# Attention and a gated feed-forward on one core: another written-out order, another table of engines, and a table of filler products

## The chip, the cores and the metric

One Trainium2 chip, one of its cores. A core has TensorE (products into PSUM, with its weight loads), VectorE, ScalarE, GpSimd and SyncE; here SyncE's queue issues all transfers between memory and SBUF. The metric is the device time of one execution in microseconds.

## What is computed

Four batches of causal attention with 12 heads, 448 positions and 64 features a head, and behind it a gated feed-forward that also mixes positions:

```
scores = q @ k^T / 8, masked above the diagonal;  attn = softmax(scores);  x = attn @ v   (heads side by side: 768)
h = relu(x @ w_in);  u, v = halves of h (512 each);  v_n = (v - mean) / sqrt(var + 1e-6)
v_s = w_spatial @ v_n + b_spatial (over positions);   out = (u * v_s) @ w_out
```

All inputs and the output are float32. Many operands are split into a high and a low part in a 16-bit type (or in the rounded 32-bit type), and three products of parts stand for one.

## The kernel before

The heads are taken in pairs, 24 in all, six to a batch. For a pair, q and k are loaded and turned; scores are taken; VectorE adds the mask and finds the negated maximum, ScalarE takes the exponential with its sum, the weights are normalised, turned, and multiplied with v (step kind A, "AV"), which gives a block of x^T. Pairs 0 to 9 turn q and k and the weights on TensorE in float32 (functions `qk_turn` and `wide`). Pairs 10 to 23 split q and k on VectorE, ScalarE or GpSimd (`scale_split`: a scaling in place, L513, a copy of the high part, L517, a subtract for the low part, L521 to L523), turn them with a transposing DMA and copy halves across (L849). After the sixth pair of a batch comes `ffn(b)`: per 128 positions a chain of 18 products for the half v (with ScalarE's evacuation to the tile hv at L1536, statistics on VectorE, a power on GpSimd, normalisation and split into vn at L1586 to L1595), four chains for u, four chains over positions (the spatial product wst x vn), and the output chains with w_out. A chain is cut into steps of three products (L1473). The weights w_in, w_spatial and w_out are loaded, decoded from 64-bit words and split in between.

All of it is written first as 2,496 steps in a list (`Plan.add`). Each has a number, the engine or engines it may run on with an assumed cost, the tiles it reads and writes, and a kind (T for turns, R and S for scores, A for AV, F, M and r for the feed-forward chains, X for a sum over partitions). Two tables then decide everything: `WHERE`, a letter for each step that may run on several engines, and `ORDER`, the sequence in which all steps are issued. `Plan.run` walks `ORDER`, takes tiles from small rings of buffers in that sequence (four banks ps, one px, three pf of PSUM; two qkT, two e, and so on) and keeps planned start times, in which a step of VectorE marked with `lock` and any step of GpSimd wait for one another. An engine runs its steps strictly in the sequence given.

TensorE also gets filler products (`plan.warm`, L689): a 128 x 128 by 256 product of a tile of ones into the third pf bank, whose result nobody reads. In the kernel before they are put in by planned times: while TensorE's planned time is under 46,000 ns and that bank is free, as many as fit in front of the next step. The trace has 32 of them, the last at 38.0 us.

Steps that the text names: 10 to 13 are the loads of pair 0 (q and k of either head), 72 to 75 those of pair 1; 14, 16, 18 and 20 turn pair 0's four pieces, 96 and 98 those of pair 1; 101 to 104 are the first scores of pair 0; 2373 is a subtract (L1593) for vn in the last batch.

Of the kernel before, what the change touches and what calls it, by code (L numbers as in the profile page):

```python
# [45 lines left out]
WARM, FILL = 46000, 107  # L46
# [3 lines left out]
    "AAADAAPPADAPPAPPPAPAAPDAAPAAPPAAPDPAPADDAPAADAAAPAAAPADDDAADAADAPDDDPAADAAPPAAAPDAPAPDAAADPADAPADDPAPDAAPPAAPD"  # L50
    "AAPADAPADPAPAPAPPAPAPPPPPPPAPAPADPPDAPPADPDPAPAPAPPPPAADAAAPAAADPPPPAPAPAPDDAADAAAAPDAPPDAPAPAPDAAPPDDAADAPAPA"
    "PADDAADDDAADADDAAAAAPPADSSAAAAADPDAAAAAPAAPDAADDDPDAPDAPSSPPDPPAPPDPAAAPAAAAAPPPAPAPDDDDADDAADPAPPAPADPADPAAPP"
    "SPPPPPPPPDPADPPDPADPPPDPPDDPPPAPDDPAPPPPDAPPAAPPPAPAADAPPPPPPAPAPAAAAAAAADAAPPPPDDPDPPSPPPDDDAPSPAPPPDPPSSPAAP"
    "PDPPPPADPPDDPADPPDDAADADPPPADAPPDDAAADDDA"
)
ORDER = (
# [141 lines left out]
class Plan:  # L198
# [38 lines left out]
    def run(self):  # L237
# [9 lines left out]
        busy = dict(FIRST)  # L247
        order, sent, ring, last = [], [], 0.0, None
        pool_end = dve_end = 0.0
        for n in ORDER:  # L250
            op = self.ops[n]
            e = op.at_engine
# [12 lines left out]
            if e == "PE":  # L265
                last = op.cls
                if busy[e] < WARM and (2, []) in free["pf"]:
                    now = max([busy[e], 2700] + [d.end + self.delay(d, e) if d.end else start for d in self.warm.deps])
                    while now + (fill := FILL if now > 6000 else 2 * FILL) < start - 40:
                        order.append((self.warm, e))  # L270
                        now += fill
# [1489 lines left out]
```

## Time and profile before

| | us |
|---|---|
| timed runs, median of 3 | 359.98 (358.84 to 360.11) |
| profiled execution, from its first to its last instruction | 358.6 |
| median of the timed runs above that span | 1.4 |
| TensorE busy, 2,602 products | 346.2 |
| VectorE / ScalarE / GpSimd busy | 285.9 / 268.7 / 161.6 |

The span is what the profiler saw of one execution; the timed runs are executions of their own. PE is TensorE, DVE VectorE, ACT ScalarE, POOL GpSimd, SP SyncE; SPq is SyncE's queue. A product counts as busy until its modelled end, so that two products close behind one another overlap and small gaps don't show.

### The profile page before, as it was taken

What the parts mean: (1) busy time and instruction counts of PE and PEld (TensorE: products, weight loads), DVE (VectorE), ACT (ScalarE), POOL (GpSimd) and SP (SyncE); (2) the same over time, 40 slices, a digit from 0 to 9 for tenths busy, and PEclk for the clock granted to TensorE, in tenths of its full rate; (3) what the DMA queues carried; (4) which work ended last, traced back from release to release, by engine and by line L of the source; (5) the groups of instructions that cost most, each with busy time, mean ns of one, the idle gap of its engine ahead of it and who ended that gap; (6) DMA issues with size and microseconds to landing.
All of it is one profiled execution on the core that took longest, in us unless ns stands there. A gap on an engine that the chain in (4) does not pass through costs nothing.

```text
span 358.6 us, 8098 instructions
## 1 busy us (share of the span) xinstructions
PE 346.2 (97%) x2602; PEld 225.5 (63%) x2602; DVE 285.9 (80%) x1116; ACT 268.7 (75%) x767; POOL 161.6 (45%) x223
## 2 busy tenths in 40 slices
PE   6999899999999999999999999999999999999995
PEld 5476555665555556765455579755755885555695
DVE  4899889999999999889898998987989994263420
ACT  3698899999999999888799989748789684231101
POOL 3133664337656468364374572334686710042400
PEclk9999999999999999999999999999999999999999
DMA  7959979746768999999997898997767978300014
GB/s 162 210 164 242 244 170 215 174 100 166 150 166 186 208 237 181 178 182 139 188 180 153 172 225 162 205 174 156 164 116 156 159 111 174 82 2 0 3 47 130
DMA packets 160796, 55.84 MB, mean 156 GB/s; under 512 B 155249, under 2 KB 156530, under 8 KB 160754
## 3 DMA queue, kind: packets, MB, share of 16 engines
q1 hardware_dynamic: 160754, 55.33, 74.5%
q8 instruction: 20, 0.33, 0.4%
q14 instruction: 22, 0.18, 0.1%
HBM read 26.76 MB, written 5.51 MB: 90 GB/s over the span
## 4 chain that ended last, share of the span: by engine, by line
PE 65%; DMA 10%; DVE 8%; ACT 7%; POOL 4%; issue 3%; SPq 2%; POOLq 0%; ACTq 0%; DVEq 0%
PE pf L1473 43%; PE px L1255 6%; DMA qkT<-qks 4%; PE ps L1021 3%; PE ps L934 3%; PE ps L1101 3%; ACT e L982 3%; PE ps L1102 2%; DMA et<-e 2%; PE ps L764 2%; POOL qks L523 2%; DVE ps L972 1%; DMA o<-in_moe_w_out_dram 1%; DMA wst<-wb 1%; ACT e L489 1%
## 5 line engine op out<-in xcount | busy, mean ns | idle before, releaser
L1473 PE MATMUL pf<-wi,xT 128*128 128x512 f16 (+1 forms) x360 | 61.6, 338 | 0.0
L1473 PE MATMUL pf<-xT,wi 128*128 128x448 f16 x288 | 59.3, 353 | 0.4 <-ACT hv L1536 0.4
L1124 ACT ACTIVATE ps<-ps,sm 128x384 f32<-128x384 f32 (+4 forms) x98 | 45.4, 463 | 13.2 <-DVE sm L1112 8.0
L1473 PE MATMUL pf<-wo,g 128*128 128x384 f32 x288 | 54.9, 341 | 0.0
L1213 DVE SCALAR_TENSOR_TENSOR e<-ps,sm,e 128x256 f16<-128x256 f32 (+4 forms) x98 | 46.3, 505 | 6.3 <-ACT e L489 6.3
L1473 PEld LDWEIGHTS pf<-wo,g 128*128 128x128 f32 x288 | 49.8, 188 | 2.0 <-issue 1.1
L489 ACT ACTIVATE e<-ps,sm 128x256 f16<-128x256 f32 (+4 forms) x98 | 44.3, 509 | 5.5 <-DVE sm L1146 1.9
L1112 DVE CUSTOM_DVE_ANT_0 ps<-ps,mask,sc 128x256 f32<-128x256 f32 (+4 forms) x98 | 47.2, 506 | 1.4 <-PE ps L1102 0.8
L1473 PEld LDWEIGHTS <-wi 128*128 128x128 f16 x288 | 27.4, 98 | 26.7 <-issue 3.0
L1473 PEld LDWEIGHTS <-xT 128*128 128x128 f16 (+1 forms) x360 | 27.2, 103 | 25.4 <-issue 4.7
L491 POOL TENSOR_SCALAR e<-e,sm 128x384 f32<-128x384 f32 (+3 forms) x43 | 23.8, 566 | 41.5 <-ACT e L982 13.6
L982 ACT ACTIVATE e<-ps,sm 128x256 f32<-128x256 f32 (+3 forms) x70 | 34.3, 500 | 4.6 <-DVE sm L972 2.6
L1473 PE MATMUL pf<-wst,vn 128*128 128x448 f16 (+1 forms) x176 | 36.0, 353 | 0.1
L523 POOL TENSOR_TENSOR qks<-qk,qks 112x512 f16<-112x512 f32 x21 | 24.2, 1157 | 20.3 <-ACT qks L489 8.9
L934 PE MATMUL ps<-qkT 64*128 64x128 f32 (+3 forms) x160 | 28.5, 444 | 0.9 <-ACT e L982 0.7
L1102 PE MATMUL ps<-qkT 128*64 128x256 f16 (+4 forms) x196 | 26.3, 284 | 0.4 <-DVE qkT L847 0.4
L1473 PEld LDWEIGHTS <-vn 128*128 128x128 f16 (+1 forms) x176 | 16.8, 98 | 15.2 <-issue 0.5
L1101 PE MATMUL ps<-qkT 128*64 128x256 f16 (+4 forms) x196 | 24.8, 291 | 0.9 <-DVE e L1213 0.7
L972 DVE CUSTOM_DVE_ANT_0 ps<-ps,e 128x128 f32<-128x128 f32 (+2 forms) x60 | 24.3, 441 | 1.2 <-PE ps L934 1.0
L1021 PE MATMUL ps<-ident,e 128*128 128x128 f32 x160 | 23.8, 279 | 1.3 <-POOL e L491 0.5
L1563 POOL TENSOR_TENSOR ln<-ln,mhalf 128x1 f32<-128x1 f32 (+1 forms) x16 | 10.6, 666 | 31.5 <-DVE ln L1555 26.8
L1021 PEld LDWEIGHTS ps<-ident,e 128*128 128x128 f32 x160 | 17.6, 141 | 9.1 <-issue 3.3
(168 smaller groups left out, 729.5 us busy)
## 6 DMA issues: line engine op xcount, KB each, us to landing
wb<-in_moe_w_in_dram SPq DMA_DIRECT2D x12, 512.0 KB, 4.3
vnat<-in_v_dram SPq DMA_DIRECT2D x24, 192.0 KB, 3.9
out_dram<-o SPq DMA_DIRECT2D x12, 384.0 KB, 3.0
qk<-in_k_dram SPq DMA_DIRECT2D x14, 224.0 KB, 4.0
qk<-in_q_dram SPq DMA_DIRECT2D x14, 224.0 KB, 4.2
o<-in_moe_w_out_dram SPq DMA_DIRECT2D x8, 384.0 KB, 4.1
qk<-in_q_dram SPq DMA_DIRECT2D x20, 112.0 KB, 4.8
qk<-in_k_dram SPq DMA_DIRECT2D x20, 112.0 KB, 3.6
```

The costliest lines, as they stand in the source:

```text
L489: nc.scalar.activation(out=dst, in_=src, func=AF.Copy, scale=scale)
L523: lambda e: HANDLE[e].tensor_tensor(out=dst_l(), in0=src(), in1=dst_h(), op=ALU.subtract),
L934: nc.tensor.matmul(out=at(bank)[r0:r0 + rn, o0:o0 + n], lhsT=flat32(t)[rows, q0:q0 + rn], rhs=k32(t)[rows, :n], start=True, stop=True, ski ...
L972: lambda e, ps=ps, n=n, u=u0 + u, sm=sm, o0=o0, h=h: nc.vector.tensor_tensor_reduce(out=at(ps)[:, o0:o0 + n], in0=at(ps)[:, o0:o0 + n], in ...
L982: lambda e, ps=ps, n=n, u=u0 + u, sm=sm, o0=o0, c=c: nc.scalar.activation(out=at(eb)[:, 128 * c:128 * c + n], in_=at(ps)[:, o0:o0 + n], fu ...
L1021: nc.tensor.transpose(out=at(pt)[:, 128 * i:128 * i + 128], in_=e32(at(eb))[:, c0 + i, :], identity=ident)
L1101: nc.tensor.matmul(out=o, lhsT=w, rhs=qkT[:, 2 + x, :n], start=True, stop=False)
L1102: nc.tensor.matmul(out=o, lhsT=w, rhs=qkT[:, 4 + x, :n], start=False, stop=True)
L1112: lambda e, ps=ps, n=n, u=u, sm=sm, o0=o0, m0=m0: nc.vector.tensor_tensor_reduce(out=at(ps)[:, o0:o0 + n], in0=at(ps)[:, o0:o0 + n], in1=m ...
L1124: nc.scalar.activation(out=dst, in_=src, func=AF.Exp, scale=-1.0, bias=at(sm)[:, u:u + 1], accum_out=at(sm)[:, 4 + 2 * u:5 + 2 * u],)
L1213: lambda e, part=part, src=src, sm=sm, u=u: nc.vector.scalar_tensor_tensor(out=part(1), in0=src(), scalar=at(sm)[:, 12 + u:13 + u], in1=pa ...
L1473: nc.tensor.matmul(out=o, lhsT=a(), rhs=rhs, start=(n0 + n == 0), stop=(n0 + n == len(mms) - 1), skip_group_check=len(out_ap()) > 1,)
```

## The change

It replaces the tables `WHERE` and `ORDER` by others and puts a table in place of the rule for fillers. The steps themselves, their dependencies, the rings of buffers and the rule of planned times are the same.

```diff
-WARM, FILL = 46000, 107
+FILLS = {
+    14: 3, 16: 1, 98: 1, 158: 5, 263: 5,
+}
...
-    "AAADAAPPADAPPAPPPAPAAPDAAPAAPPAAPDPAPADDAPAADAAAPAAAPADDDAADAADAPDDDPAADAAPPAAAPDAPAPDAAADPADAPADDPAPDAAPPAAPD"
...
+    "DDAAPPPAAPAAPDAPDDPAPPAAPPDAPPAAPAPDPAAADPAAAPAAPAAAPAPPDAPDAADAPDAPDPADAAPPDAPAAAPAAAPAADDPAAPPDDPAAAAAPPAAAA"
...
-                if busy[e] < WARM and (2, []) in free["pf"]:
-                    now = max([busy[e], 2700] + [d.end + self.delay(d, e) if d.end else start for d in self.warm.deps])
-                    while now + (fill := FILL if now > 6000 else 2 * FILL) < start - 40:
-                        order.append((self.warm, e))
-                        now += fill
+                if n in FILLS and (2, []) in free["pf"]:
+                    order += [(self.warm, e)] * FILLS[n]
```

Read out of the two pairs of tables: 197 steps run on another engine.

| steps on | before | after |
|---|---|---|
| VectorE | 932 | 910 |
| ScalarE | 547 | 546 |
| GpSimd | 228 | 248 |
| SyncE | 210 | 213 |
| TensorE (without fillers) | 579 | 579 |

The moves are 42 steps from ScalarE to GpSimd and 33 back, 39 from VectorE to ScalarE and 29 back, 30 from VectorE to GpSimd and 19 back, and five with SyncE. Beginning of two engines' sequences:

| | before | after |
|---|---|---|
| SyncE | 10, 73, 72, 75, 74, 12, 11, 13, 26, 22 | 73, 10, 12, 11, 13, 75, 95, 72, 22, 74 |
| TensorE | 14, 96, 98, 16, 18, 20, 101, 102, 103, 104, 105 | 14, 16, 18, 20, 101, 102, 103, 104, 96, 98, 105 |

A number in `FILLS` is that of the step in front of which the fillers stand. The first score step of a pair is TensorE's step number 123 (pair 8), 301 (pair 16), 400 (pair 20) and 466 (pair 23) before, and 114, 295, 384 and 454 after. From one TensorE step to the next the kind changes 203 times before and 179 times after; from F to A, R, S or M 22 times before and 12 after.

## Rows read from the trace of the kernel before

**Rows 1.** stretches of the span: busy us of each engine (instructions), TensorE clock, DMA

```profile
0.00:40.00 40.00, 35.28 (x264) 24.33 (x264) 31.80 (x135) 28.69 (x93) 12.76 (x39) 1.00 0.85 198
40.00:180.00 140.00, 136.50 (x1028) 81.60 (x1027) 128.27 (x515) 130.20 (x379) 76.18 (x100) 1.00 0.86 179
180.00:310.00 130.00, 129.97 (x1051) 88.43 (x1049) 108.69 (x433) 100.56 (x283) 61.67 (x72) 1.00 0.85 163
310.00:358.60 48.60, 44.48 (x265) 31.17 (x262) 17.09 (x35) 9.24 (x17) 11.03 (x14) 0.99 0.10 33
sum 358.60, PE 346.23 PEld 225.53 DVE 285.86 ACT 268.69 POOL 161.63; mean PE 86.56 PEld 56.38 DVE 71.46 ACT 67.17 POOL 40.41
```

**Rows 2.** TensorE's waits: who for whom, us in total, times, longest

```profile
PE ps L764 <- DMA qk<-in_k_dram: 1.0, 1, 1.0
...
PE pf L1473 <- ACT hv L1536: 0.4, 1, 0.4
```

**Rows 3.** timeline of TensorE at the start: start, us, line, tile, count, idle before

```profile
3.17 0.93 PE L738 MATMUL ps<-ident,qk 112*64 112x112 f32 x4 [1.31 <-DMA qk<-in_q_dram]
3.88 0.85 PE L689 MATMUL pf<-ones 128*128 128x256 f16 x3
4.59 0.98 PE L764 MATMUL ps<-ident,qk 112*128 112x112 f32 x4
...
8.88 0.77 PE L738 MATMUL ps<-ident,qk 112*128 112x112 f32 x4
9.49 0.27 PE L689 MATMUL pf<-ones 128*128 128x256 f16 x1
9.69 2.38 PE L934 MATMUL ps<-qkT 64*128 64x128 f32 x12
12.74 0.97 PE L934 MATMUL ps<-qkT 64*64 64x448 f32 x4 [0.68 <-ACT e L982]
13.65 0.50 PE L689 MATMUL pf<-ones 128*128 128x256 f16 x3
```

**Rows 4.** timeline of SyncE's queue at the start

```profile
0.80 1.46 SPq L701 DMA_DIRECT2D qk<-in_q_dram  x3
...
4.43 0.49 SPq L701 DMA_DIRECT2D qk<-in_k_dram  x1
```

**Rows 5.** DMA issues from 0 to 20 us: count, KB, us to landing

```profile
qk<-in_q_dram SPq DMA_DIRECT2D x8, 112.0 KB, 2.8
qk<-in_k_dram SPq DMA_DIRECT2D x6, 112.0 KB, 3.1
```

**Rows 6.** timeline of TensorE, a chain before half-array and before other products

```profile
53.35 0.81 PE L1473 MATMUL pf<-wi,xT 128*128 128x512 f16 x3
54.09 1.69 PE L934 MATMUL ps<-qkT 64*128 64x128 f32 x12
...
64.20 0.81 PE L1473 MATMUL pf<-wi,xT 128*128 128x512 f16 x3
64.85 0.93 PE L764 MATMUL ps<-ident,qk 112*128 112x112 f32 x8
```

**Rows 7.** the lines of subtract and copy on either engine: ns min/median/max

```profile
L523 POOL TENSOR_TENSOR qks<-qk,qks x21: 1147/1157/1164, 100.2 to 273.4; 112x512 f16<-112x512 f32 x21
...
L523 DVE TENSOR_TENSOR qks<-qk,qks x7: 674/682/920, 99.2 to 244.2; 112x512 f16<-112x512 f32 x7
...
L491 POOL TENSOR_SCALAR qks<-qk x8: 617/618/626, 142.0 to 258.6; 112x512 f16<-112x512 f32 x8
...
L487 DVE TENSOR_SCALAR qks<-qk x7: 417/421/1399, 133.8 to 272.9; 112x512 f16<-112x512 f32 x7
```

**Rows 8.** timeline of GpSimd and VectorE, two subtracts of the last batch

```profile
317.55 1.15 POOL L1595 TENSOR_TENSOR vn<-hv,vn 128x512 f16<-128x512 f32 x1 [0.94 <-DVE vn L487]
317.56 1.69 DVE L1595 TENSOR_TENSOR vn<-hv,vn 128x512 f16<-128x512 f32 x1
...
322.88 0.69 DVE L1595 TENSOR_TENSOR vn<-hv,vn 128x512 f16<-128x512 f32 x1
```

More of the change, by code (lines that the diff above doesn't have):

```diff
@@ L49 @@
 WHERE = (
-    "AAADAAPPADAPPAPPPAPAAPDAAPAAPPAAPDPAPADDAPAADAAAPAAAPADDDAADAADAPDDDPAADAAPPAAAPDAPAPDAAADPADAPADDPAPDAAPPAAPD"
[L51 to L54, printed above, removed]
+    "DDAAPPPAAPAAPDAPDDPAPPAAPPDAPPAAPAPDPAAADPAAAPAAPAAAPAPPDAPDAADAPDAPDPADAAPPDAPAAAPAAAPAADDPAAPPDDPAAAAAPPAAAA"
+    "ADDDAPPAAPAPAPAPPPPAPPPPPAPPPADAAPPAAPPADPAPAPAPAPPPPAADAAPPAAADPPAPPPAPPPADAAAAADAADAPPADPDADPADAPADAAADDPADA"
+    "AAADAPDDPAAAAADAAAADPPPDSSPPAAAPAAAAAPAAAPADAAPDDPAADPADSSPAPPPPPPPPPPPPAAAAAPPDPPDPPPAADAAADDAAPPPPSAPADPPDPP"
+    "SPPPPPPPAPPDPPDAPDPAPPPADPSAAPDPDDDSSAPPDPPPAPPPDAPDAAAPPDPDPPPPDAAAAADPPPPAPPPPPPPPPPSPAPPPPPPPPAAAPPPPSSPPPP"
+    "PPDPAAADPPADADPAADPDADAAPADPPPDPPDDAAAAAA"
 )
 ORDER = (
[127 rows of a table removed]
[128 rows of a table added]
 )
```

255 rows, old and new, of the table ORDER are left out of this document.

## The prediction

> **What bounds the kernel now.** I read the stretches of the span first, because the share of busy time differs from stage to stage. TensorE is busy for 346.2 of 358.6 us, and its idle 12.4 us lie in three places [rows 1]: 4.7 us before 40 us, 3.5 us in the 140 us from 40 to 180, 0.03 us from 180 to 310, and 4.1 us after 310, most of which is the last copy and store behind the last product. From 40 to 180 us ScalarE is busy 130.2 and VectorE 128.3 of 140 us, so there three engines run nearly full side by side; from 180 on TensorE alone is full. GpSimd has room everywhere (161.6 us busy in all). So a new sequence can gain only what TensorE loses: its start, the time between products of different kinds (busy in the profile, but not streaming), and its waits. Work taken off VectorE after 180 us is worth nothing by itself.
>
> Next the list of TensorE's waits, to see that no single one is large: 1.0 us for a k load near 39 us, 0.4 us for ScalarE's hv at 319 us [rows 2]. Then the first microseconds in the timeline [rows 3]. The first q transpose starts at 3.17 us, the second group only at 4.59, and the first score product of pair 0 at 9.69. Between stand the turns of pair 1 (steps 96 and 98) with fillers before them, and only then the other three turns of pair 0. Three fillers take 0.85 us at 3.88 and 0.50 us at 13.65: in the first ten microseconds TensorE streams at the lower level (1.2 GHz), afterwards at 2.4, although the clock column of rows 1 prints 1.00 for the whole stretch.
>
> **The change part by part.**
>
> *The start.* SyncE issues its first eight loads 0.49 us apart (1.46 us for three) [rows 4]. In the old order pair 0's four loads are the 1st, 6th, 7th and 8th, the last issued at 4.43 us; in the new one they are the 2nd to 5th, the last at about 0.80 + 4 x 0.5 = 2.8 us. They land 2.8 us (q) and 3.1 us (k) after their issue [rows 5], so the last of the four at about 5.9 us. The new order of TensorE turns pair 0 alone (14, 16, 18, 20), with one filler between where before there were nine and two turns of pair 1. A turn of four products takes about 0.75 us at the lower level (0.77 with its tail at 8.88 us). So the fourth turn starts near 6.2 and ends near 7.0, and the first scores start at about 7.2 us instead of 9.69: 2.5 us earlier. Not all of it stays. The twelve products of 101 to 104 took 2.38 us at the higher level [rows 3]. If the clock rises at the same 9.4 us (the filler at 9.49 is the first short one, 0.27 us), the first 2.2 us of them run at half pace and do 1.1 us of the work; the rest ends at 9.4 + 1.3 = 10.7 instead of 12.07 us. That is 1.4 us earlier. Bounds: 2.5 us gained if VectorE's reading of the scores is what counts, and 1.2 us lost if the clock stays low until 20 us (a rival, below). I take a gain of 1.5 us. It goes through to the end because everything up to 40 us hangs on this first softmax: the two turns of pair 1 then fill TensorE's wait for it (0.68 us idle at 12.74 and fillers at 13.65) instead of standing in front.
>
> *The fillers.* 32 before, 15 after. A filler is free where the next product waits anyway. At the higher level one costs 0.11 us (three in 0.50 us with a tail of 0.27). All 17 dropped ones in the way would be 17 x 0.11 = 1.9 us, none in the way 0. They stand in front of products that wait, so I take 0.3 us.
>
> *Changes of kind.* Decoded from the two orders, TensorE changes from one kind of step to another 203 times before and 179 times after. Three 512-column products of a chain followed by transposes start the next thing after 0.65 us (64.20 to 64.85); followed by score products on half the rows, after 0.74 us (53.35 to 54.09) [rows 6]: 0.09 us for such a change, nothing for the other. Changes from a full chain to half-array steps (scores, AV, the narrow hv chain) fall from 22 to 12: 10 x 0.09 = 0.9 us. Bounds: nothing, and 24 x 0.09 = 2.2 us if every change costs that. I take 0.9.
>
> *Work moved between engines.* VectorE runs 22 steps fewer, GpSimd 20 more, ScalarE 1 fewer, SyncE 3 more. With the medians of each form on each engine (the like of rows 7) VectorE loses 13 us of work, GpSimd gains 22, ScalarE loses 1. A subtract in qks is 0.68 us on VectorE and 1.16 on GpSimd; the f16 copy before it 0.42 and 0.62 [rows 7]. From 40 to 180 us, where it could matter, ScalarE's load stays the same within 0.5 us and VectorE's falls by some 4 of 128: relief, but ScalarE is as full as before, so I count 0. Above 180 us TensorE hides it. The three extra across copies on SyncE are one issue of about 0.5 us each in a queue that mostly waits; 0, and 1.5 us at worst.
>
> *The shared port.* At 317.56 us VectorE's subtract takes 1.69 us beside a GpSimd subtract that began at 317.55, and 0.69 us without one at 322.88 [rows 8]. ScalarE's hv, and with it TensorE at 319, comes late by it: the 0.4 us of rows 2. The new table gives this subtract (step 2373) to GpSimd. I count the 0.4 us as gone. The GPSIMD Engine Reference of the Trainium skill (section 8, Key points) says that GpSimd shares its SBUF interfaces with VectorE and contends with instructions that have two SBUF inputs. The trace agrees by the 1.69 us, and the rule speaks against 22 us more of GpSimd's work; if each microsecond held VectorE up, VectorE would end with 9 us more and not 13 less, still below TensorE's total, and the sum would stay.
>
> *Other waits.* The 3.5 us idle between 40 and 180 us can go, or come again at other places, for nearly every product there has new neighbours: between -3.5 and +3.5 us. I take 0.
>
> Sum against the profiled span: 358.6 - 1.5 - 0.3 - 0.9 - 0.4 = 355.5 us. The median of the timed runs is 1.4 us above that span (359.98), so 356.9 us.
>
> **The rivals.**
>
> *New waits eat the gain (no change).* The new order brings attention forward: the first score step of pair 20 is TensorE's step 384 instead of 400, of pair 8 step 114 instead of 123. ScalarE must deliver the same exponentials earlier while it is 93% busy from 40 to 180 us [rows 1]. For it: only some 10 us of idle ScalarE to draw on. Against it: from 180 us on, products of the feed-forward part cover TensorE without a gap. If TensorE waits 3 us more between 40 and 180, the time is 359.9 us.
>
> *The clock stays low (no change).* With 5 fillers instead of 11 in the first 9.5 us, and otherwise transposes, the higher level may come later. Between 9.69 and 20 us TensorE did about 7 us of real products; at half pace from 7.2 us on they take 14 and end at 21.2, so the start is 1.2 us late instead of 1.5 early: 356.9 + 2.7 = 359.6 us. Slower than before by more than can be told only if the low level lasted to about 24 us. Against it: in rows 3 the level rose after a stretch that was mostly transposes. The page TensorE: Matmul & The Clock Gate of the Trainium skill (Part 4) says that transposes do not count as TensorE's activity; by it the rise would wait for the score products, which start at 7.2 us here. No row separates the two, since fillers and transposes alternate.
>
> *GpSimd becomes late (slower).* For pairs 19 to 21 the new table puts nearly the whole splitting of q and k on GpSimd. With rows 7 one pair's copies and subtracts for q and k cost 2 x (0.62 + 1.16) = 3.6 us there, 2 x (0.42 + 0.68) = 2.2 on VectorE, plus the scaling: about 1.8 us later per pair, in a queue where the normalising of others stands behind. Then comes a transposing DMA, then the scores. If the cover before the scores is shorter than that, TensorE waits: four pairs at 1.8 us are 7 us, 356.9 + 7 = 364 us. For it: GpSimd's forms are half as fast, and its share from 180 to 310 us goes from 47% to about 57%. Against it: TensorE waits 0.03 us there now, with long chains between. It decides from where the pair's operands land after its score step is due.
>
> That the change does less than it says (no filler, because the third feed-forward bank is taken at those steps) costs nothing in this sum.
>
> **How the numbers follow.** Forecast 0.58; new waits 0.16 and the clock 0.09, both no change; GpSimd late 0.13; other mishaps of the new neighbours, slower, 0.04. What a measurement here can tell from no change is about 0.5%, 1.8 us. Faster 0.58, within 0.25, slower 0.17. The range: below, all of the start (2.5), the changes of kind (2.2) and some of the idle 3.5 us give 353.3; above, the no-change cases and one pair's worth of lateness, 359.9 + 1.8 = 361.7. The forecast's own range is 353.3 to 358.2.
>
> **What would show it.** Right: the first half-array score product near 7.2 us; TensorE's busy total some 2 to 3 us smaller; no wait at the spatial products of the last batch; VectorE near 273 us and GpSimd near 184 us busy; TensorE without a gap from 180 to 310 us. Wrong: fillers or transposes at the low pace after 12 us; waits of scores for qkT between 200 and 290 us; more than 5 us idle from 40 to 180 us, ended by ScalarE.

## The result, and the profile after

| | before | after |
|---|---|---|
| median, us | 358.73 (357.02 to 361.51) | 361.49 (359.08 to 363.98) |
| timed executions | 19 | 19 |

The ratio is 1.0071 with a 95% interval of 1.0054 to 1.0089: slower by 0.7%, some 2.5 us. A second comparison on another occasion gave 1.0066 (1.0045 to 1.0088). I had forecast 356.9 us, faster, with 0.17 for slower. That 361.49 us lies inside the range that I gave (353.3 to 361.7) is no merit: its upper end stood for one pair's worth of lateness of GpSimd in splitting q and k, which did not happen.

The two first profiles mislead: the span fell from 358.6 to 358.0 us. A timed execution lasts some 1.8 us longer than its span (360.98 with a span of 359.2, 357.29 with 355.4), so the profiled execution of before was one of the longest of its kernel and that of after one of the shortest. Executions of one kernel differ by some 2 us either way, so a difference of 0.7% is not to be read from one pair of spans; below I use several profiles of each side.

Two of the stretches of the changed kernel and the sums, in the columns of [rows 1]:

```profile
40.00:180.00 140.00, 136.35 (x1033) 83.60 (x1030) 132.34 (x510) 131.95 (x384) 84.76 (x108) 1.00 0.86 185
180.00:310.00 130.00, 129.01 (x1043) 87.79 (x1041) 104.06 (x422) 95.99 (x274) 65.35 (x80) 1.00 0.85 159
...
sum 358.00, PE 345.49 PEld 226.06 DVE 282.31 ACT 267.83 POOL 174.64; mean PE 86.37 PEld 56.51 DVE 70.58 ACT 66.96 POOL 43.66
```

From 40 to 180 us VectorE rose by 4.1, ScalarE by 1.8 and GpSimd by 8.6 us; I had VectorE fall there. More profiles confirm VectorE (128.3 to 129.5 us busy in three profiles of the old tables, 131.8 to 133.1 in four of the changed ones) and not ScalarE (130.2 to 132.5 against 131.4 to 132.5: the same). From 180 to 310 TensorE, gapless before, lacks 1.0 us. TensorE's longest wait after the start, from the answer to [rows 2]:

```profile
PE px L1255 <- DVE xT L1277: 0.7, 1, 0.7
```

Several of half a microsecond follow it. But the kernel before has such waits too, beside the two in rows 2:

```profile
PE ps L1101 <- DVE e L1213: 0.7, 2, 0.3
PE ps L1021 <- POOL e L491: 0.5, 1, 0.5
```

The places are new and the sizes are not: from 40 to 180 us TensorE is idle 3.65 us (140 - 136.35), before 3.50. The start, the answer to [rows 3], TensorE with its weight loads (PEld) and then ScalarE:

```profile
3.93 0.93 PE L738 MATMUL ps<-ident,qk 112*64 112x112 f32 x4 [1.82 <-POOL e L650]
4.64 0.42 PE L689 MATMUL pf<-ones 128*128 128x256 f16 x1
4.86 2.67 PE L738 MATMUL ps<-ident,qk 112*64 112x112 f32 x12
7.46 3.62 PE L934 MATMUL ps<-qkT 64*128 64x128 f32 x12
...
11.15 0.61 PEld L764 LDWEIGHTS ps<-ident,qk 112*128 112x128 f32 x4 [1.22 <-ACT e L982]
11.99 0.39 PEld L764 LDWEIGHTS ps<-ident,qk 112*128 112x128 f32 x4 [0.17 <-ACT e L982]
12.55 0.20 PEld L934 LDWEIGHTS ps<-qkT 64*64 64x64 f32 x4 [0.17 <-ACT e L982]
10.19 0.47 ACT L982 ACTIVATE e<-ps,sm 128x256 f32<-128x256 f32 x1 [2.08 <-DVE sm L972]
...
11.83 0.58 ACT L982 ACTIVATE e<-ps,sm 128x384 f32<-128x384 f32 x1
...
14.40 0.63 ACT L982 ACTIVATE e<-ps,sm 128x448 f32<-128x448 f32 x1 [0.48 <-DVE sm L993]
```

And ScalarE in the kernel before:

```profile
11.78 0.37 ACT L982 ACTIVATE e<-ps,sm 128x128 f32<-128x128 f32 x1 [2.29 <-DVE sm L972]
...
12.14 0.47 ACT L982 ACTIVATE e<-ps,sm 128x256 f32<-128x256 f32 x1
...
14.60 0.64 ACT L982 ACTIVATE e<-ps,sm 128x448 f32<-128x448 f32 x1
```

Pair 0's scores start at 7.46 us (forecast 7.2) and its first exponential 1.59 us earlier than before (10.19 against 11.78). Its last one, over 448 columns, starts only 0.20 us earlier (14.40 against 14.60). The lead goes at TensorE. A turn or a score needs one of the four ps banks, and pair 0's first scores hold them until ScalarE's exponentials give them back. Before, the 448-wide scores took the first bank that came free, behind the second exponential (12.14 + 0.47 us; they start at 12.74, rows 3). Now the two turns of pair 1 stand in front of them and take the first two banks, at 11.15 and 11.99, and the scores get the third, behind the fifth exponential (11.83 + 0.58 us): they start at 12.55, 0.19 us earlier than before. From there to their exponential it is 1.85 us, before 1.86. ScalarE's copies of pair 1's turns (0.98 us at 12.38) are not on this path: behind them ScalarE stands 0.48 us for VectorE. Of the lead that I counted as lasting to the end little is left within 5 us.

The stall at 319 us [rows 2, 8] is gone. GpSimd has both subtracts now, 4 us apart (316.70 and 320.67), and TensorE's first wait there is 0.22 us, for a third one:

```profile
316.70 1.15 POOL L1595 TENSOR_TENSOR vn<-hv,vn 128x512 f16<-128x512 f32 x1 [2.07 <-DVE vn L487]
...
320.67 1.15 POOL L1595 TENSOR_TENSOR vn<-hv,vn 128x512 f16<-128x512 f32 x1
...
323.84 1.12 PE L1473 MATMUL pf<-wst,vn 128*128 128x448 f16 x5 [0.22 <-POOL vn L1595]
```

What the stall hung on I had read wrongly. ScalarE's hv in the kernel before started when GpSimd's own subtract ended (317.55 + 1.15 = 318.70 us), not with VectorE's slowed one (317.56 + 1.69 = 319.25):

```profile
318.74 0.69 ACT L1536 ACTIVATE hv<-pf,inv 128x512 f32<-128x512 f32 x1 [1.21 <-POOL vn L1595]
```

**VectorE beside GpSimd.** The slowing itself matters elsewhere. Around 41 us GpSimd of the changed kernel splits w_in, and VectorE's normalising copy of a 128x128 block of e takes 1.17 us beside it (GpSimd and then VectorE); the same form takes 0.27 us in the kernel before, at 22.97 (second block):

```profile
41.37 3.53 POOL L523 TENSOR_TENSOR wi<-wa,wi 128x512 f16<-128x512 f32 x3
40.73 0.84 DVE L487 TENSOR_SCALAR wi<-wa 128x512 f16<-128x512 f32 x1
41.48 1.17 DVE L487 TENSOR_SCALAR e<-e,sm 128x128 f32<-128x128 f32 x1
42.58 0.67 DVE L1277 SCALAR_TENSOR_TENSOR xT<-px,vsc,xT 128x448 f16<-128x448 f32 x1
```

```profile
22.97 0.27 DVE L487 TENSOR_SCALAR e<-e,sm 128x128 f32<-128x128 f32 x1
```

With the copy before it (0.84 us, a form that otherwise takes 0.42) VectorE loses 1.3 us there, and its next result, xT, is what TensorE waits for 0.69 us at 43.30. All nine profiles with the changed tables up to 75 us have these two slow copies, none of the six with the old tables there has. For the stretch from 40 to 180 us I counted each instruction of VectorE at the median of its form in the old tables (the sums exceed the stretch, as instructions overlap). So counted, its work fell from 167.4 to 163.5 us (means of three and four profiles), as forecast; but what its instructions took above these medians rose from 0.9 to 5.9 us, all of it in instructions during which GpSimd worked.

**Where the time goes.** Both kernels do the same steps on TensorE in other orders, so I compare the times at which the same amount of work is done: each step counts with the 15th percentile of the intervals from such a step to the next, over the kernels compared. The rows say how much later than in one profile of the kernel before with 15 fillers (span 355.5) a stretch of work is passed. The first three kernels have the old tables, the last four the changed ones (those named hoist have some products of TensorE moved; see below).

| TensorE's work, us (time in the run) | before | 15 fillers | hoist_8 | after | again | hoist_early4 | hoist_7 | new tables minus old, means |
|---|---|---|---|---|---|---|---|---|
| 0 to 60 (to 75 us) | 1.17 | 0 | -0.97 | 1.49 | 2.16 | 2.56 | 1.62 | +1.9 |
| 60 to 145 (75 to 170) | 0.83 | 0 | 0.32 | -1.21 | -0.49 | -1.11 | -0.25 | -1.1 |
| 145 to 180 (170 to 205) | 0.92 | 0 | 0.76 | 2.03 | 1.91 | 2.32 | 1.84 | +1.5 |
| 180 to 320 (205 to 350) | 0.13 | 0 | 0.25 | 0.01 | -0.05 | 0.01 | -0.01 | -0.1 |

The sum, +2.2 us, is about what the two ratios say (2.5 and 2.4 us). The changed tables lose by 75 us, win back half of it by 170, lose again to 205, and from there nothing changes. All the profiles below, counted the same way, bear out the first loss: six with the old tables up to 75 us lie between -1.0 and 1.2, nine with the changed ones between 1.4 and 2.6. On average the changed ones are 0.7 us ahead at 18 us, 0.5 behind at 27 and still at 41, 1.0 behind at 43, right after the slow copies, and 1.7 at 75. The loss from 170 to 205 is less sure: seven profiles with old tables there lie between 0 and 1.2, ten with changed ones between 1.2 and 2.3, 0.9 apart on average.

### The profile page after: what moved, and what is told of

It reads as the page before. It is cut to its first block, busy times and chain, and to the rows that moved or that the text cites. A ratio compares the mean times of both kernels' runs of the same rounds, so it can differ in the third digit from the quotient of the medians.

```text
span 358.0 us, 8072 instructions
## 1 busy us (share of the span) xinstructions
PE 345.5 (96%) x2585; PEld 226.1 (63%) x2585; DVE 282.3 (79%) x1094; ACT 267.8 (75%) x766; POOL 174.6 (49%) x243
## 3 DMA queue, kind: packets, MB, share of 16 engines
HBM read 26.76 MB, written 5.51 MB: 90 GB/s over the span
## 5 line engine op out<-in xcount | busy, mean ns | idle before, releaser
L1473 PE MATMUL pf<-xT,wi 128*128 128x448 f16 x288 | 58.5, 353 | 0.0
L1124 ACT ACTIVATE ps<-ps,sm 128x256 f32<-128x256 f32 (+4 forms) x98 | 45.4, 463 | 16.6 <-DVE sm L1112 9.7
L1473 PE MATMUL pf<-wo,g 128*128 128x384 f32 x288 | 54.0, 340 | 0.0
L1213 DVE SCALAR_TENSOR_TENSOR e<-ps,sm,e 128x384 f16<-128x384 f32 (+4 forms) x98 | 45.3, 505 | 7.1 <-ACT e L489 6.9
L489 ACT ACTIVATE e<-ps,sm 128x384 f16<-128x384 f32 (+4 forms) x98 | 44.3, 509 | 3.5 <-DVE sm L1146 2.7
L491 POOL TENSOR_SCALAR e<-e,sm 128x128 f32<-128x128 f32 (+3 forms) x43 | 23.1, 549 | 36.0 <-DVE sm L993 15.4
L982 ACT ACTIVATE e<-ps,sm 128x128 f32<-128x128 f32 (+3 forms) x70 | 34.2, 499 | 6.2 <-DVE sm L972 5.4
L934 PE MATMUL ps<-qkT 64*128 64x128 f32 (+3 forms) x160 | 30.1, 463 | 0.3 <-ACT e L982 0.2
L523 POOL TENSOR_TENSOR qks<-qk,qks 112x512 f16<-112x512 f32 x22 | 26.2, 1200 | 8.6 <-DVE qks L487 4.4
```

The lines of the kernel that those rows point to most:

```text
L489: nc.scalar.activation(out=dst, in_=src, func=AF.Copy, scale=scale)
L523: lambda e: HANDLE[e].tensor_tensor(out=dst_l(), in0=src(), in1=dst_h(), op=ALU.subtract),
L934: nc.tensor.matmul(out=at(bank)[r0:r0 + rn, o0:o0 + n], lhsT=flat32(t)[rows, q0:q0 + rn], rhs=k32(t)[rows, :n], start=True, stop=True, ski ...
L982: lambda e, ps=ps, n=n, u=u0 + u, sm=sm, o0=o0, c=c: nc.scalar.activation(out=at(eb)[:, 128 * c:128 * c + n], in_=at(ps)[:, o0:o0 + n], fu ...
L1124: nc.scalar.activation(out=dst, in_=src, func=AF.Exp, scale=-1.0, bias=at(sm)[:, u:u + 1], accum_out=at(sm)[:, 4 + 2 * u:5 + 2 * u],)
L1213: lambda e, part=part, src=src, sm=sm, u=u: nc.vector.scalar_tensor_tensor(out=part(1), in0=src(), scalar=at(sm)[:, 12 + u:13 + u], in1=pa ...
```

## The experiments

All ratios are to the kernel before, timed on the same chip between the runs.

**The changed kernel again, and the fillers.** Theory: the tables bring new waits. Rival: with fewer fillers the clock rises late.

```diff
 before_newfill: the tables of before, with
-WARM, FILL = 46000, 107
+FILLS = {14: 3, 16: 1, 98: 1, 158: 5, 263: 5}
 after_fill14: the changed kernel, with
-    14: 3, 16: 1, 98: 1, 158: 5, 263: 5,
+    14: 11, 16: 3, 98: 1, 158: 5, 263: 5,
 after_oldrule: the changed tables, with the old rule (WARM, FILL) in place of FILLS: 80 fillers
 after_fillers_before: the changed tables, with the 32 fillers of before at the same steps
+FILLS = {14: 1, 96: 3, 98: 3, 16: 1, 18: 1, 20: 1, 101: 1, 157: 3, 158: 3, 159: 7, 137: 1, 194: 2, 261: 1, 263: 2, 291: 1, 49: 1}
```

> The changed kernel once more, for a second profile and more timed runs. If its loss lies in a start that differs from run to run (the clock theory), the span of this profile lies some 2 to 4 us above the first one of 358.0 us, the fillers and turns of the first 15 us run at the low pace for longer, and from 40 us on the steps stand at the same distances as in the first profile. If the loss is spread over waits between 40 and 310 us (the theory of new waits), the start is the same and the later steps come later by 2 to 3 us. Ratio to the kernel before: 1.005 to 1.009 by both.

> The tables of the kernel before, with only the 15 fillers of the new table (3, 1, 1, 5, 5 in front of the steps 14, 16, 98, 158, 263) in place of the 32. Clock theory: TensorE does less between 3 and 9.5 us, the higher level comes later, and the kernel is slower by 1 to 3 us (ratio 1.003 to 1.008). Theory of new waits: fillers stand in idle time, ratio 0.998 to 1.002.

> The changed tables with the old rule for fillers, which puts 80 of them into this order, 12 of these in front of or among the first eight TensorE steps. Clock theory: the higher level comes sooner and more surely, ratio to the kernel before 0.995 to 1.002 if the fillers behind 10 us cost little. Theory of new waits: ratio 1.005 to 1.010 as for the change, or more by what the added fillers stand in the way (0.11 us each, 7 us for all).

> The changed kernel with 11 fillers instead of 3 before its first turn and 3 instead of 1 before the second, so that TensorE is busy nearly without a gap from 1.3 us on. Clock theory: the higher level comes in the first score products or before them in most runs; ratio to the kernel before 0.996 to 1.003. Theory of new waits: ratio 1.005 to 1.009, like the change.

> The changed kernel with the 32 fillers of the kernel before, ahead of the same products of TensorE as there (14, 96, 98, 16, 18, 20, 101, 157, 158, 159, 137, 194, 261, 263, 291, 49), instead of its 15. In the kernel before, the exchange of 32 for 15 cost 0.9 us. If it costs as much here: 0.9 us faster than the changed kernel. If fillers only cost their own time where they delay a product that is ready: 0.5 to 1 us slower, as with 80 fillers (4 us).

| | us | ratio (95%) |
|---|---|---|
| after_again | 360.53 | 1.0066 (1.0045 to 1.0088) |
| before_newfill | 359.28 | 1.0025 (1.0003 to 1.0048) |
| after_oldrule, 80 fillers | 364.86 | 1.0187 (1.0164 to 1.0209) |
| after_fill14, 25 fillers | 361.12 | 1.0098 (1.0061 to 1.0136) |
| after_fillers_before, 32 fillers | 362.38 | 1.0089 (1.0066 to 1.0111) |

With ten fillers more at the first turns, the twelve scores run at the higher level, 2.26 instead of 3.62 us:

```profile
7.82 2.26 PE L934 MATMUL ps<-qkT 64*128 64x128 f32 x12
...
14.26 0.63 ACT L982 ACTIVATE e<-ps,sm 128x448 f32<-128x448 f32 x1 [0.64 <-DVE sm L993]
```

The 448-wide exponential starts at 14.26 instead of 14.40 us, and the kernel is not faster. The clock rival falls: the slow scores are real (the higher level came only about 4 us after their start) and cost nothing that these runs show. The first exponential starts 0.37 us earlier (9.82 against 10.19), but the 448-wide scores only 0.14 us earlier (12.41 against 12.55), for pair 1's second turn stands in front of them, and its k load, issued at 5.51, lands at 11.8 (the profile puts that turn's wait down to an exponential that had ended by 11.6). From these scores to their exponential it is 1.85 us again. The page TensorE: Matmul & The Clock Gate of the Trainium skill (Part 4: transposes are no activity) agrees with these two starts: sixteen products of turns with one filler among them, behind three fillers and 1.8 us of idling, left the level low; behind eleven fillers and 0.45 us of idling and with three fillers among them they did not. As the idling differs too, the two starts don't single the transposes out. Fewer fillers are not the whole loss: they cost 0.25% in the old sequence (interval to 0.48%) of 0.7%, and in the changed sequence more of them bring none of it back.

**Which part of the tables.** Cuts: the first N entries of one sequence with its engines, then all other steps in the order and on the engines of the other kernel. The fillers are those of the kernel that starts.

```diff
 frontN_after (N = 300, 690, 1075: to 42, 91, 138 us); frontN_before the other way round
-ORDER = OLD
+ORDER = NEW[:N] + [n for n in OLD if n not in NEW[:N]]
 WHERE: each step's letter from the kernel whose part of the order it stands in
 seq_before_eng_after: ORDER and fillers of before, with
-WHERE = OLD
+WHERE = NEW
```

> The first 690 entries of the sequence (to about 91 us) with their engines and the 15 fillers from the changed kernel, the other 1,810 entries and their engines from the kernel before. The kernel before is 358.0 here and the changed one 360.5. Theory 1, local waits in two places (28 to 60 us of TensorE's work, and 140 to 180): this part holds the first of them, 1.3 us, and 0.3 us at the start: 359.6. Theory 2, the start's waits are handed on and set off everything later: 360.5. Theory 3, the late half alone loses: 358.0 to 358.4.

> The other way round: the first 690 entries, their engines and the 32 fillers from the kernel before, the rest from the changed one. Theory 1 (two local places): only the late one is left, about 1 us, and 0.3 gained near the end: 358.9. Theory 2 (the start's waits handed on): 358.0. Theory 3 (the late half alone): 360.3.

> The first 1,075 entries (to about 136 us) from the kernel before with engines and fillers, the rest from the changed one. Theory 1: the waits at 175 to 205 us are in this rest, 1 to 1.3 us, but the 1.5 us that the changed kernel wins between 118 and 165 us are partly left out: 359.0. Theory 2: 358.0. Theory 3: 360.3.

> The whole sequence and the fillers of the kernel before, the engines of the changed one. If the loss comes from which engine does a step: 360 or more. If it comes from the sequence alone: 358.0. If each table only fits the other of its own pair: slower than both kernels, 362 and more, with new waits of TensorE on VectorE, ScalarE or GpSimd all over.

> Only the first 300 entries (to about 42 us) with their engines and the 15 fillers from the changed kernel; the rest from the kernel before. With 690 entries it was 2.5 us over the kernel before. If the early loss is made by 42 us (VectorE then stands 0.2 to 0.9 us for a weight load that lands at 35.8 us, and ends its casts a microsecond later): 2 to 2.5 us over again. If it is made from 45 to 75 us, where ScalarE is 98.6% busy in the changed kernel and 95% before: 0.5 to 1 us over, which is what the new fillers alone cost.

> The first 1,075 entries (to about 138 us) from the changed kernel, the rest from the kernel before: the stretch of 165 to 205 us is that of the kernel before. If the loss has two places, an early one and one of 1.3 us at 165 to 205 us: 1.2 us over the kernel before, that is 1.2 us faster than the changed one. If all of it is early and the late waits only follow from it: 2.5 us over, as the changed kernel.

> The first 1,625 entries (to about 206 us) from the kernel before, the rest from the changed one. In the traces nothing is lost after 205 us. If so: as the kernel before, within 0.3 us, or 0.2 to 0.4 us faster by the wait at 319 us that is gone. If the changed end (15 steps of VectorE and 12 of ScalarE given to GpSimd) is dear: 1 us over or more.

> The first 300 entries (to about 42 us), their engines and the 32 fillers from the kernel before, the rest from the changed one. If the loss of the changed kernel is in its start: 1.2 us faster than the changed one, 1.1 us over the kernel before. If the parts only fit their own other half: no faster than the changed one, 2.3 us over the kernel before or more.

| cut at | changed part first | changed part behind |
|---|---|---|
| 300 entries, 42 us | 360.21, 1.0039 (1.0018 to 1.0060) | 361.89, 1.0083 (1.0058 to 1.0108) |
| 690, 91 us | 361.09, 1.0072 (1.0052 to 1.0093) | 362.70, 1.0125 (1.0105 to 1.0145) |
| 1,075, 137 us | 365.18, 1.0153 (1.0120 to 1.0187) | 360.85, 1.0066 (1.0045 to 1.0086) |
| 1,625, 206 us | | 360.96, 1.0059 (1.0036 to 1.0081) |
| sequence before, engines after | 379.70, 1.0609 (1.0576 to 1.0643) | |

The parts don't add. At 690 they make 0.72 + 1.25 = 2.0%, the whole 0.7%. A cut can bring waits of its own at the seam; the one at 1,075 with the changed part first shows it as a single wait, between 130 and 160 us:

```profile
PE ps L1102 <- DVE qkT L847: 2.9, 1, 2.9
```

My theory of two local losses fails as a sum, most of all with front300_before, which should have won 1.2 us and won nothing, front1075_after (1.5% slower instead of 0.3) and front1625_before (0.6% slower instead of nothing, with its loss behind the seam). Two things hold: the changed start brings no gain (1.0039, with its lower bound above 1, of which its 15 fillers may be 0.0025), and the new table of engines is worth nothing on the old sequence (+6%; the new sequence with the old engines was not run).

**Filling the waits.** If the new waits of TensorE are themselves the loss, products that were ready before a wait began should fill it.

```diff
 after_hoist_early4: in ORDER, a product moved to just before the one that waits
+587 before 303, 588 before 428, 515 before 565, 606 before 375
 after_hoist_late3
+722 before 1074, 1208 before 1573, 1611 before 1684
 after_hoist_7: both
 before_hoist_8: in the ORDER of before
+349 before 440, 619 before 375, 649 before 662, 663 before 940, 664 before 935, 694 before 1098, 719 before 1074, 1172 before 1516
```

> The changed kernel with four products of TensorE moved to just before a product that waits, each of them ready before that wait began: 587 before 303 (wait of 0.68 us at 43 us), 588 before 428 (0.63 us at 50), 515 before 565 (0.31 us at 66), 606 before 375 (0.68 us at 87). Nothing else differs. The changed kernel was 2.5 us over the kernel before. If these waits cost what they last, the products fill them (0.65, 0.63, 0.2 and 0.65 us): 2.0 us faster than the changed kernel. If the chains of ScalarE and VectorE set the pace there (ScalarE 94% busy from 40 to 180 us), the wait only comes a product later: within 0.3 us of the changed kernel.

> The changed kernel with three products moved ahead in the same way: 722 before 1074 (waits of 0.52 and 0.42 us at 156 us), 1208 before 1573 (0.38 and 0.34 us at 182 to 183), 1611 before 1684 (0.63 us at 193). If the waits cost what they last: 0.55 + 0.57 + 0.4 = 1.5 us faster than the changed kernel. If VectorE and ScalarE set the pace: within 0.3 us of it.

> Both sets of moves, seven products. If each wait costs what it lasts: 3.5 us faster than the changed kernel, which is 1 us faster than the kernel before. If an early gain is handed on but the later waits end at times that other engines set: as the early four alone. If other engines set the pace all along: as the changed kernel.

> The kernel before with eight of its products moved ahead of waits of its own in the same way: 349 before 440 (0.71 us), 619 before 375 (0.63), 649 before 662 (0.30), 663 before 940 (0.50), 664 before 935 (0.41), 694 before 1098 (1.25 in the profiled execution, not in others), 719 before 1074 (0.35), 1172 before 1516 (0.27). The other half of the same question. If waits cost what they last: 2.5 to 3 us faster than the kernel before. If other engines set the pace: within 0.3 us of it. If the kernel before has such waits as large as the changed one's and they cost it nothing, the waits of the changed kernel are not the reason of its loss.

Measured: early four 361.76, 1.0099 (1.0068 to 1.0129); late three 361.32, 1.0081 (1.0056 to 1.0106); all seven 360.58, 1.0063 (1.0038 to 1.0088), where 3.5 us were to be gained if each wait cost what it lasts; before_hoist_8 359.16, 1.0008 (0.9990 to 1.0026), where it was 2.5. Nothing is gained on either side. TensorE in the changed kernel at the first of the waits:

```profile
43.30 2.04 PE L1255 MATMUL px<-et,vnat 128*64 128x448 f32 x14 [0.69 <-DVE xT L1277]
...
46.08 0.55 PE L1021 MATMUL ps<-ident,e 128*128 128x128 f32 x3
46.46 0.81 PE L1473 MATMUL pf<-wi,xT 128*128 128x512 f16 x3
47.11 1.57 PE L1021 MATMUL ps<-ident,e 128*128 128x128 f32 x12
48.52 0.93 PE L764 MATMUL ps<-ident,qk 112*128 112x112 f32 x8
```

and with the seven moves:

```profile
42.74 0.82 PE L1473 MATMUL pf<-wi,xT 128*128 128x512 f16 x3
43.52 2.04 PE L1255 MATMUL px<-et,vnat 128*64 128x448 f32 x14
...
46.30 2.61 PE L1021 MATMUL ps<-ident,e 128*128 128x128 f32 x15
48.74 0.93 PE L764 MATMUL ps<-ident,qk 112*128 112x112 f32 x8
```

The 0.69 us are gone. But the fifteen turns of weights behind now take 2.61 us where they took 0.55 + 1.57: their weight loads stand 1.0 us for ScalarE's exponentials and 0.5 us for GpSimd's normalising. The chain product had filled that time at 46.46. The next step starts 0.22 us later, not 0.65 earlier. That is how VectorE and ScalarE stand there too: xT starts at 42.80 instead of 42.58 and the 448-wide exponential at 47.48 instead of 47.25, and VectorE's slow copy takes 1.17 us as before. The wait of TensorE was the form in which the pace of VectorE and ScalarE showed, not the cause.

That ScalarE has next to no room from 45 us on, the stretches of the changed kernel say:

```profile
45.00:75.00 30.00, 29.39 (x239) 18.39 (x237) 28.61 (x108) 29.60 (x98) 16.05 (x24) 1.00 0.70 169
165.00:210.00 45.00, 44.04 (x343) 24.30 (x341) 38.78 (x158) 37.05 (x105) 26.92 (x34) 1.00 1.02 187
```

and those of before:

```profile
45.00:75.00 30.00, 29.46 (x231) 18.10 (x227) 27.34 (x103) 28.60 (x90) 14.05 (x22) 1.00 0.72 168
165.00:210.00 45.00, 44.66 (x351) 24.89 (x349) 40.53 (x162) 40.49 (x115) 23.58 (x28) 1.00 0.97 173
```

From 45 to 75 us ScalarE is busy 29.60 of 30 us (28.60 before) and VectorE 28.61 (27.34). From 165 to 210 it is the other way: ScalarE and VectorE have less to do, 37.1 and 38.8 against 40.5 and 40.5, GpSimd has 26.9 against 23.6, and TensorE 0.6 us less.

**GpSimd in the second stretch.** TensorE's weight loads wait for GpSimd's vn near 198 us, which they don't in the kernel before. Six splits of vn given back:

```diff
 after_split_back: WHERE of the changed kernel, but
-1138, 1153, 1168, 1183, 1184, 1185 on GpSimd
+1138, 1168 on VectorE; 1153, 1183, 1184, 1185 on ScalarE (as before)
```

> The changed kernel with six steps that split the normalised rows of the spatial products of the second batch (1138, 1153, 1168, 1183, 1184, 1185) on the engines of the kernel before (four on ScalarE, two on VectorE) instead of GpSimd; the sequence is the changed one. TensorE's weight loads wait 0.5 to 1.1 us for GpSimd there at 198 us. If GpSimd's lateness makes the loss of 165 to 205 us: 0.6 to 1.2 us faster than the changed kernel. If ScalarE and VectorE set the pace there anyway: no faster, or slower.

Measured: 368.66 us, 1.0250 (1.0214 to 1.0287), 1.8% above the changed kernel. The waits grow and move to other engines: from 202 to 208 us TensorE waits 1.24 us for VectorE's sc, 0.69 and 0.99 us for GpSimd's vn and 0.58 us for ScalarE's.

So giving these six steps back wins nothing; with this sequence they are better on GpSimd. What else GpSimd does there was not varied.

## Why the prediction was wrong

*What failed first: "It goes through to the end because everything up to 40 us hangs on this first softmax."* The 1.5 us were there (1.59 at the first exponential), and 0.2 were left at the last exponential of the same pair. TensorE's wait that the two turns of pair 1 were to fill was a wait for a ps bank, and the turns don't only fill it: they take the first two banks that come free, so that the 448-wide scores get the third and start 0.19 us earlier than before instead of 1.5. front300_after gives the sign: with the changed start alone the kernel is 0.39% slower (its 15 fillers included), not 1.5 us faster. I had also not seen that the first turn begins later (3.93 instead of 3.17 us; pair 0's first load is now issued second, at 1.25 us, and lands at 3.79; the row names a step of GpSimd that ends just then, the second profile names the load), which the scores at 7.46 still made good.

*What failed next: the shared port, "the sum would stay", and VectorE's load, "VectorE's falls by some 4 of 128: relief".* I took the slowing of VectorE beside GpSimd as 0.4 us at one place and looked only at VectorE's total. From 40 to 180 us VectorE's work at its usual durations did fall by some 4 us, but beside GpSimd, with 8.6 us more there, its instructions grew by 5 us, and VectorE ended busier (132.3 us against 128.3) in the stretch where TensorE hangs on it. At 41 us this is 1.3 us in front of the result that TensorE waits for, in every profile of the changed tables. That this slowing makes the loss is shown for that one wait in the traces; no run took GpSimd's work away there. For ScalarE the sentence ("the same within 0.5 us") holds over several profiles, though the first pair shows +1.8.

*What failed in size: other waits, "I take 0", with bounds of 3.5 us either way.* Against the old tables the stretches of work passed by +1.9, -1.1, +1.5 and -0.1 us, +2.2 us net, the lead of the start included. Little of it shows as idle time of TensorE (3.65 against 3.50 us from 40 to 180). The rival "New waits eat the gain" named the mechanism (attention brought forward onto a full ScalarE) and the stretch from 40 to 180 us, but at 0.16, and priced as no change; since there was no gain to eat, it came out slower.

*Fillers, -0.3:* a gain was forecast; 17 fewer cost 0.9 us in the old sequence (bounds 0.1 to 1.7). *Changes of kind, -0.9:* no row shows this gain, and no run tested it alone; TensorE's busy total, which was to fall by 2 to 3 us, is 345.5 and 344.9 in two profiles of the changed kernel and 343.5 in the old tables with the same 15 fillers. *The port at 319 us, -0.4:* the wait (0.38 us) is gone and one of 0.22 us stands in its place; and it had not hung on VectorE's slow subtract. Over the whole kernel VectorE's work at the medians fell by some 11 us, but what its instructions took above them rose by some 3 us (5 us from 40 to 180, less behind it) beside 13 us more of GpSimd: the GPSIMD Engine Reference of the Trainium skill (section 8, Key points: contention of the two engines) agrees. The totals were mis-sized: VectorE 282.3 us busy (forecast 273), GpSimd 174.6 (184).

*The rivals:* GpSimd late for pairs 19 to 21 did not happen; nothing is lost after 205 us, and the 1.0 us that TensorE lacks from 180 on lie before 200. The clock stays low did happen in part (scores of 3.62 us, the low level until about 11.7 us and not to 21) and cost nothing that the runs show.

*The base:* the sum was made against 358.6 us as if it were typical; the median execution of before has a span of about 358.7 - 1.8 = 356.9 us, so 355.5 us of span would have been a gain of 1.4 us and not of 3.1.

*What stays open.* Shown: most of the loss is in the tables and none was found in the clock; TensorE's new waits can be filled without gain; the changed start gains nothing, and why; VectorE is held up beside GpSimd; the loss arises by 75 us and, less surely, again from 170 to 205 us. That VectorE and ScalarE set the pace is shown in the traces for the first of the filled waits, at 43 us. How much of the loss comes from VectorE's slowing, and which steps of the tables bring the rest, is not shown: no run moved GpSimd's work at 41 us, and a cut adds waits of its own. No version tried beats the kernel before.

## What to carry to other kernels

Where three engines run at 90% and more, a wait of one engine is the place where another's pace shows: before counting an earlier start or a filled wait as gain, follow the same pair to its last instruction. Work that is moved into a wait takes buffers too: ask who gets the next one. Before work goes to GpSimd, ask which instructions of a full VectorE will run beside it. A written-out order and its table of engines belong together; the old order with the new engines was 6% slower. For a difference under 1%, take several executions of each side before reading one pair of profiles.

## What the runs showed of the hardware

The granted clock fell in the middle of a run. In after_split_back TensorE was busy 0.87, 0.91 and 0.71 us of each 2 us from 202 to 208 us, and over the next 4 us the granted clock was 0.51 and 0.63:

```profile
202.00:204.00 2.00, 0.87 (x5) 0.25 (x3) 1.57 (x9) 2.00 (x6) 0.00 (x0) 1.00 0.57 111
204.00:206.00 2.00, 0.91 (x3) 0.21 (x3) 1.33 (x8) 2.00 (x8) 1.78 (x2) 1.00 0.90 172
206.00:208.00 2.00, 0.71 (x3) 0.31 (x4) 0.14 (x2) 2.00 (x7) 1.90 (x3) 1.00 1.12 207
208.00:210.00 2.00, 2.00 (x8) 0.82 (x6) 1.91 (x7) 1.73 (x7) 0.11 (x1) 0.51 0.34 72
210.00:212.00 2.00, 2.00 (x9) 0.82 (x8) 2.00 (x7) 1.39 (x5) 1.52 (x1) 0.63 0.00 0
```

Nine products of 448 columns took 3.20 us there (0.36 each) and six took 1.31 (0.22 each) at 201.56. These waits so cost twice: by themselves, and by the lower level (1.2 GHz) behind them.

VectorE is slower beside GpSimd, and by how much differs: a copy of 128x128 took 1.17 us instead of 0.27, a subtract of 128x512 1.69 instead of 0.69, a copy of 128x512 0.84 instead of 0.42 us.
